# Spreading the weights of four V pairs by one set of copies in a decode kernel

## The chip, the cores and the metric

The kernel runs on one core of one Trainium2 chip. The metric is device time in microseconds (us) of one execution. Executions of one kernel agree within about 0.1% (before: 1342.69 to 1343.98 us). The profiles abbreviate the engines: PE is TensorE, PEld its weight loads, DVE is VectorE, ACT is ScalarE, POOL is GpSimd, SP is SyncE, which issues the loads. L516 is line 516 of the kernel that ran, so the same line has other numbers in other kernels.

## The reference, cut to what matters

One decode step of attention over a long cache is mixed with a small MLP. What matters here is the attention:

```python
# k_cache, v_cache: 4 batches x 32 heads x 8192 keys x 128, bf16: 268 MB each
scores = jnp.einsum("bhqd,bhkd->bhqk", q, k_cache) * (Dh ** -0.5)
p = _softmax(scores, axis=-1)
o = jnp.einsum("bhqk,bhkd->bhqd", p, v_cache)
```

Each byte of K and V is used once. Everything else (`wq`, `wo`, the MLP weights) is some 39 MB.

## The kernel before

The work is cut into 32 "pairs" of K and 32 of V. One pair is four heads of one batch, 8.39 MB, loaded into two of the five slots of a ring. Eight pairs make a group, which has one softmax. The V pairs run eight pairs behind the K pairs, so in the long middle part TensorE alternates: a K pair, a V pair, a K pair, and so on. Behind the last K pair, the last eight V pairs follow one another.

```python
order = []
for d in range(ND):
    order += [("k", d)] + [("v", d - LAG)] * (d >= LAG)
order += [("v", d) for d in range(ND - LAG, ND)]
```

In the profiles `TB` holds transposed K (the work of VectorE), `S_ps` the scores, `o_ps` the sums of the V matmuls and `OS` a scaled copy of them, which ScalarE begins behind every second V pair ("the OS activation").

The softmax of a group leaves its exponentials, transposed, in the tile `PT`. They are the weights of the V matmuls, but a V matmul needs them in a wide, mostly zero layout. The tile `PB` holds that layout for four V pairs (`NW = 4` slots), and `spread_p` copies one pair's weights from `PT` into its slot, with two copies on ScalarE and two on GpSimd:

```python
def spread_p(d):
    g, t = divmod(d, GD)                      # group, pair in the group (GD = 8)
    lo = RD * (d % NW)                        # slot of PB
    Pv = PT_t[g][:, :, RD * t:RD * t + RD].rearrange("p (q j) i -> p i q j", j=4)
    Bv = PB[:, lo:lo + RD].rearrange("p i z w s j -> p i (z w) s j")
    for q in range(NQ):
        at = slice(QP * q, QP * (q + 1))
        if q % 2 == 0:
            nc.scalar.copy(out=Bv[at, :, :, q, :], in_=Pv[at])
        else:
            nc.gpsimd.tensor_copy(out=Bv[at, :, :, q, :], in_=Pv[at])
```

Behind a softmax it is called for three pairs of the new group (four for the first). In `v_pair`, a slot is filled again as soon as its V pair is done, for the pair that comes four later:

```python
def v_pair(d):
    ...                                        # cut: load of V, 64 matmuls with PB[slot d % NW]
    if tv == GV - 1:
        sum_up(d, g, t, b, h0)
    if t < GD - NW:
        spread_p(d + NW)
    if t == GD - 1 and d + 1 < ND:
        spread_p(d + NW)
```

## Time and profile before

| | before |
|---|---|
| time, median of 6 runs | 1343.07 us (1342.69 to 1343.98) |
| bytes read, mean rate | 575.68 MB, 429 GB/s |
| busy share of the DMA queue that loads | 99.6% of 16 engines |
| TensorE, VectorE busy | 1050.9 us (78%), 638.2 us (48%) |
| ScalarE, GpSimd busy | 66.2 us, 71.4 us (5% each) |
| of these the copies of `spread_p` | 39.6 us, 38.9 us (64 copies on each) |

The table is read from the bottom: the edited operations are 3% of the span on each of two engines that idle 95% of it. The lines themselves are shown in the prediction.

### The profile page before, as it was taken

The page shows a single profiled execution, that of the slowest core. Times are in us where ns is not written, and L with a number is a line of the kernel's source. Part 1 is how long each engine was busy: PE and PEld are TensorE (multiplying, and loading weights), DVE is VectorE, ACT ScalarE, POOL GpSimd, SP SyncE. Part 2 cuts the span into 40 slices and gives each one's busy share as a digit, 9 for nine tenths or more (in the row PEclk, how much of TensorE's full clock was granted, in tenths as well). Part 3 has the DMA queues.
Part 4 walks back from the last instruction along what each step waited for, and adds up shares of the span by engine and source line. Part 5 has one row for each costly group of instructions (what it writes and reads, how often), then busy time and mean ns, then how long its engine had stood idle before and what let it go on. Part 6 is the DMA issues. An engine that isn't in the chain of part 4 may idle for free.

```text
span 1341.0 us, 6872 instructions
## 1 busy us (share of the span) xinstructions
PE 1050.9 (78%) x4550; PEld 138.3 (10%) x1396; DVE 638.2 (48%) x386; ACT 66.2 (5%) x99; POOL 71.4 (5%) x209
## 2 busy tenths in 40 slices
PE   2665877887778788787879778789697879898888
PEld 0000000001001010101001010101011011111111
DVE  2555988556544347454436256646145556100000
ACT  0000000200000000100000000100000000111000
POOL 2000000100000001000000000100000000100000
PEclk9687999898988998888989898899898889889899
DMA  9999999999999999999999999999999999999998
GB/s 415 438 430 435 436 436 424 441 429 428 436 434 428 443 430 423 442 429 435 434 435 428 433 438 434 436 421 431 434 434 438 434 421 440 432 426 431 426 427 340
DMA packets 15466, 576.13 MB, mean 430 GB/s; under 512 B 1726, under 2 KB 1990, under 8 KB 3148
## 3 DMA queue, kind: packets, MB, share of 16 engines
q1 hardware_dynamic: 15428, 575.69, 99.6%
q8 instruction: 23, 0.38, 0.1%
q14 instruction: 7, 0.06, 0.0%
q10 hardware_dynamic: 8, 0.00, 0.0%
HBM read 575.68 MB, written 0.01 MB: 429 GB/s over the span
## 4 chain that ended last, share of the span: by engine, by line
DMA 62%; DVE 24%; PE 12%; another core or an unknown queue 1%; issue 0%; ACT 0%; SPq 0%; DVEq 0%
DMA ring<-in_A_k_cache_dram 51%; DVE TB L456 21%; PE o_ps L540 9%; DMA ring<-in_A_v_cache_dram 7%; DMA ring<-in_A_wo_dram 2%; DVE OS L561 2%; DMA x<-in_gate_w_dram 2%; PE S_ps L461 1%; PE acc L286 1%; DVE mx L483 0%; PE S_ps L320 0%; PE led L577 0%; PE o_ps L320 0%; DVE PT L497 0%
## 5 line engine op out<-in xcount | busy, mean ns | idle before, releaser
L456 DVE STREAM_TRANSPOSE TB<-ring 128x2048 uint32<-128x2048 uint32 x256 | 568.2, 2278 | 474.2 <-DMA ring<-in_A_k_cache_dram 467.1
L461 PE MATMUL S_ps<-TB,Z 128*128 128x512 bf16 x1990 | 524.3, 412 | 198.1 <-DVE TB L456 183.9
L540 PE MATMUL o_ps<-ring,PB 128*64 128x512 bf16 x2048 | 465.1, 389 | 49.8 <-DMA ring<-in_A_v_cache_dram 48.5
L461 PEld LDWEIGHTS <-Z 128*128 128x128 bf16 x512 | 53.0, 103 | 654.4 <-issue 654.4
L540 PEld LDWEIGHTS <-PB 128*64 128x64 bf16 x512 | 57.4, 112 | 450.9 <-issue 450.3
L516 POOL COPY PB<-PT 32x256 bf16<-32x256 bf16 x64 | 38.9, 608 | 711.3 <-PE o_ps L540 518.4
L569 DVE SCALAR_TENSOR_TENSOR OS<-o_ps,mE,OS 128x512 f32<-128x512 f32 x5 | 3.8, 751 | 139.1 <-ACT OS L567 139.1
L514 ACT COPY PB<-PT 32x256 bf16<-32x256 bf16 x64 | 39.6, 619 | 256.6 <-PE o_ps L540 250.7
L438 POOL COPY Z<-qa 32x4 bf16<-32x4 bf16 x128 | 25.6, 200 | 459.5 <-PE S_ps L461 433.3
L557 ACT ACTIVATE OS<-o_ps,mE 128x512 f32<-128x512 f32 x11 | 7.6, 687 | 451.9 <-PE o_ps L540 451.9
L561 DVE SCALAR_TENSOR_TENSOR OS<-o_ps,mE,OS 128x512 f32<-128x512 f32 x33 | 24.3, 737 | 1.5
L492 ACT ACTIVATE TB<-S_ps,mx 128x2048 bf16<-128x2048 f32 x4 | 7.9, 1967 | 332.0 <-DVE mx L489 332.0
L244 PE MATMUL S_ps<-identb,x 6*128 6x6 bf16 x8 | 0.6, 196 | 22.1 <-DMA x<-in_gate_w_dram 22.1
L286 PE MATMUL acc<-ring,hT 128*4 128x512 bf16 x56 | 13.6, 408 | 5.4 <-ACT TB L492 5.4
L286 PE MATMUL acc<-ring,LT 128*4 128x512 bf16 x64 | 15.1, 378 | 1.6 <-DMA ring<-in_A_wo_dram 1.0
L320 PE MATMUL o_ps<-ring,xw 128*4 128x512 bf16 x112 | 9.8, 471 | 4.9 <-DMA ring<-in_B_w_gate_dram 4.9
L577 PEld LDWEIGHTS o_ps<-selg,OS 128*128 128x128 f32 x88 | 11.5, 191 | 9.4 <-issue 9.0
L497 DVE STREAM_TRANSPOSE PT<-TB 128x2048 bf16<-128x2048 bf16 x4 | 9.2, 2312 | 6.4 <-ACT TB L492 6.4
L483 DVE TENSOR_REDUCE mx<-S_ps 128x1 f32<-128x2048 f32 x4 | 9.1, 2282 | 6.2 <-PE S_ps L461 6.2
L577 PE MATMUL o_ps<-selg,OS 128*128 128x8 f32 x88 | 10.5, 245 | 0.0
L567 ACT ACTIVATE OS<-o_ps,mE 128x512 f32<-128x512 f32 x5 | 3.4, 687 | 128.2 <-PE o_ps L540 128.2
L589 DVE SCALAR_TENSOR_TENSOR OT<-led,sgb,rinv 128x8 bf16<-128x8 f32 x5 | 1.2, 237 | 16.2 <-PE led L577 16.2
(73 smaller groups left out, 81.8 us busy)
## 6 DMA issues: line engine op xcount, KB each, us to landing
ring<-in_A_v_cache_dram SPq DMA_DIRECT2D x18, 4096.0 KB, 30.0
ring<-in_A_k_cache_dram SPq DMA_DIRECT2D x14, 4096.0 KB, 29.8
ring<-in_A_v_cache_dram SPq DMA_DIRECT2D x6, 2048.0 KB, 39.5
ring<-in_B_w_gate_dram SPq DMA_DIRECT2D x1, 7168.0 KB, 37.0
ring<-in_B_w_up_dram SPq DMA_DIRECT2D x1, 7168.0 KB, 37.1
ring<-in_B_w_down_dram SPq DMA_DIRECT2D x1, 7168.0 KB
ring<-in_A_wo_dram SPq DMA_DIRECT2D x4, 1024.0 KB
ring<-in_A_v_cache_dram SPq DMA_DIRECT2D x4, 1024.0 KB, 30.3
```

Source lines behind the costliest of these rows:

```text
L286: nc.tensor.matmul(acc(n), lhsT=lhsT, rhs=rhs, start=start, stop=True, skip_group_check=True)
L320: nc.tensor.matmul(ps[32 * k:32 * k + Bn, z, :], lhsT=xT[TW * half + t], rhs=cols(w, t, 4 * z + k), start=(half + t == 0), stop=(half == 1 ...
L438: nc.gpsimd.tensor_copy(out=Z[at, :, QP - 1 + QP * q], in_=qa[at, :, h0 + q, b])
L456: nc.vector.transpose(out=flat_t.bitcast(U32).rearrange("p (j i) -> p j i", j=CJ), in_=kn[:, half].bitcast(U32))
L461: nc.tensor.matmul(sps[:, z, :], lhsT=Z[:, 2 * half + e, s:s + P], rhs=T[:, 16 * z:16 * z + 16, :, e], start=(t + n + half + e == 0), stop ...
L483: nc.vector.tensor_reduce(out=mx[:, 0:1], in_=sps[:].rearrange("p z n -> p (z n)"), axis=AX.X, op=ALU.max)
L497: nc.vector.transpose(out=PT[:].rearrange("p j i -> p (j i)"), in_=PTs)
L514: nc.scalar.copy(out=Bv[at, :, :, q, :], in_=Pv[at])
L516: nc.gpsimd.tensor_copy(out=Bv[at, :, :, q, :], in_=Pv[at])
L540: nc.tensor.matmul(o_ps[w // 2][row:row + NM, w % 2, :], lhsT=PB[:, RD * (d % NW) + n, z].rearrange("p w s j -> p (w s j)"), rhs=vn[:, j0 ...
L561: nc.vector.scalar_tensor_tensor(out=OS[:], in0=o_ps[w // 2][:, w % 2, :], scalar=mE[:, w:w + 1], in1=OS[:], op0=ALU.mult, op1=ALU.add)
L577: nc.tensor.matmul(oT, lhsT=OS[:, q * Dh:(q + 1) * Dh], rhs=selg[:, q].rearrange("p t s -> p (t s)"), start=(q == 0), stop=(q == 3), skip_ ...
```

## The change

The intent is fewer, larger copies. While K pairs still come, the weights of four V pairs are spread by one set of four copies: behind the first softmax, then behind the fourth and the eighth V pair of a group, when all four slots are free. Behind the last K pair, where no K pair lies between two V pairs, they are still spread pair by pair, except that the first three go together and the last two go together.

```diff
-            for i in range(NW):
-                if g == 0 or i < NW - 1:
-                    spread_p(GD * g + i)
+            if g == 0:
+                spread_p(0, NW)
+            elif g == NG - 1:
+                spread_p(GD * g, NW - 1)
...
-    def spread_p(d):
+    def spread_p(d, n=1):
...
-        Pv = PT_t[g][:, :, RD * t:RD * t + RD].rearrange("p (q j) i -> p i q j", j=4)
-        Bv = PB[:, lo:lo + RD].rearrange("p i z w s j -> p i (z w) s j")
+        Pv = PT_t[g][:, :, RD * t:RD * (t + n)].rearrange("p (q j) i -> p i q j", j=4)
+        Bv = PB[:, lo:lo + RD * n].rearrange("p i z w s j -> p i (z w) s j")
...
-            if q % 2 == 0:
+            if q % 2 == 0 and not (q and n == NW - 1):
...
-        if t < GD - NW:
-            spread_p(d + NW)
-        if t == GD - 1 and d + 1 < ND:
-            spread_p(d + NW)
+        if g == NG - 1:
+            if t < 2:
+                spread_p(d + NW)
+            if t == 3:
+                spread_p(d + NW - 1, 2)
+        elif t == NW - 1:
+            spread_p(d + 1, NW)
+        elif t == GD - 1:
+            if g + 1 < NG - 1:
+                spread_p(d + 1, NW)
+            else:
+                spread_p(d + NW)
```

More of the change, by code (lines that the diff above doesn't have):

```diff
@@ L146 @@
     NW = GD // 2
+    NG = ND // GD
     HV = GV * NQ
```

## The prediction

> **What bounds the kernel now.** I read the page from the top: busy shares first, then the strip of the span, the DMA queues and the chain, then the groups of the lines that the change edits, and last the timeline around the copies.
>
> ```profile
> PE 1050.9 (78%) x4550; PEld 138.3 (10%) x1396; DVE 638.2 (48%) x386; ACT 66.2 (5%) x99; POOL 71.4 (5%) x209
> DMA  9999999999999999999999999999999999999998
> GB/s 415 438 430 435 436 436 424 441 429 428 436 434 428 443 430 423 442 429 435 434 435 428 433 438 434 436 421 431 434 434 438 434 421 440 432 426 431 426 427 340
> q1 hardware_dynamic: 15428, 575.69, 99.6%
> HBM read 575.68 MB, written 0.01 MB: 429 GB/s over the span
> DMA 62%; DVE 24%; PE 12%; another core or an unknown queue 1%; issue 0%; ACT 0%; SPq 0%; DVEq 0%
> ```
>
> The reader is to see that no compute engine is near full, while the DMA digit is 9 in every slice but the last, and one queue is busy for 99.6% of 16 engines' span. The bytes are fixed: 575.69 MB at 429 GB/s over the span are 1341 us, the span itself. The table by stretches agrees: every stretch I asked for up to 1330 us has a DMA share of 1.00 or 1.01, only the last 11 us have 0.48. So the kernel streams the K and V caches, and time comes down only if the stream gets faster or its last 11 us shorter.
>
> The chain puts 24% on VectorE and 12% on TensorE, which looks like something to win. It isn't. The chain follows what set each transfer's issue: a ring slot came free, the queue issued, the data landed some 30 us later. One pair is 4 heads x 8192 x 128 x 2 B = 8.39 MB, or 19.5 us at 430 GB/s; of 30 us to landing, about 10 us are spent behind an older transfer. The issue was thus about 10 us early, and moving it by less costs nothing. ScalarE has 0% of this chain, and GpSimd does not appear in it.
>
> The edited lines:
>
> ```profile
> L516 POOL COPY PB<-PT 32x256 bf16<-32x256 bf16 x64 | 38.9, 608 | 711.3 <-PE o_ps L540 518.4
> L514 ACT COPY PB<-PT 32x256 bf16<-32x256 bf16 x64 | 39.6, 619 | 256.6 <-PE o_ps L540 250.7
> L438 POOL COPY Z<-qa 32x4 bf16<-32x4 bf16 x128 | 25.6, 200 | 459.5 <-PE S_ps L461 433.3
> L540 PE MATMUL o_ps<-ring,PB 128*64 128x512 bf16 x2048 | 465.1, 389 | 49.8 <-DMA ring<-in_A_v_cache_dram 48.5
> ```
>
> Each V pair has four copies, two on ScalarE and two on GpSimd: 32 x 2 = 64 on each, 39.6 and 38.9 us busy. They wait for TensorE (PB frees when the V matmuls are done); the V matmuls wait for the V data (48.5 of their 49.8 us idle). One view puts 8.0 us of two V weight loads, at 1181.3 and 1249.2 us, down to these GpSimd copies; but those had ended at 1150.0 and 1202.2, and the same two loads also wait for V data, which the matmuls behind them show (3.10 and 2.74 us). The timeline shows why the copies are hidden:
>
> ```profile
> 678.88 14.00 PE L540 MATMUL o_ps<-ring,PB 128*64 128x512 bf16 x64
> 692.94 1.23 POOL L516 COPY PB<-PT 32x256 bf16<-32x256 bf16 x2 [33.70 <-PE o_ps L540]
> 693.07 1.24 ACT L514 COPY PB<-PT 32x256 bf16<-32x256 bf16 x2
> 720.01 14.00 PE L540 MATMUL o_ps<-ring,PB 128*64 128x512 bf16 x64
> ```
>
> The columns are start, duration, engine, what. One V pair ends at 692.9, its copies take 1.2 us, and the next V pair starts at 720.0, because the order alternates: a K pair lies between.
>
> [...] of eight GpSimd copies at 241.6 us (5.22 us, 0.65 each), beside VectorE's transposes, none took noticeably longer, while one copy of the 64 took 973 ns; at 1145.6 a VectorE cast of x lies beside six copies that need 4.27 us[...].
>
> **The change part by part.** The instruction order that both kernels build to shows it: ACT falls from 47 rows to 41, POOL from 63 to 56, and TensorE, VectorE and the DMA queue keep their sequences, row for row. On TensorE only waits differ: up to V pair 20 the weight loads now wait for ACT and POOL ahead of pairs 0, 4, 8, 12, 16 and 20, where before they did ahead of 0, 8 and 16 (and for ACT ahead of 1, 9 and 17).
>
> *Steady part (V pairs 0 to 23).* Removed: 24 x 4 copies of 256 elements per partition. Added: six sets (after the first softmax and behind V pairs 3, 7, 11, 15, 19), each of four copies of 1024. [...] GpSimd: the 16-element copy of line 438 takes 200 ns and the 256-element one 608, so (608 - 200) / 240 = 1.70 ns per element, and 200 + 1.70 x 1008 = 1.91 us each. ScalarE: 48 x 0.62 = 29.8 us become 12 x 1.91 = 22.9. GpSimd: 48 x 0.61 = 29.2 become 22.9.
>
> *Last group (V pairs 24 to 31).* Behind the last softmax three pairs are spread at once: one copy of 768 on ScalarE (1.5 us), three on GpSimd (3 x 1.5 = 4.5 us, where six took 4.27). Pairs 27, 28 and 29 stay as they are; 30 and 31 go together behind V pair 27 (two copies of 512 on each engine, 1.04 us each). ScalarE: 9.9 us become 1.5 + 3.7 + 2.1 = 7.3. GpSimd: 9.7 become 4.5 + 3.7 + 2.1 = 10.3.
>
> Sum: ScalarE 39.6 to about 30.2 us, GpSimd 38.9 to about 33.2. None of it is on the path that sets the end, so the direct gain is 0 us.
>
> *What becomes tighter.* Between V pairs 3 and 4, say, four pairs' weights used to be ready long before; now the set starts when V pair 3 ends, and V pair 4 needs it. ScalarE has the OS activation first (0.69 us), then two copies: 0.69 + 2 x 1.91 = 4.5 us. The gaps in TensorE's V matmuls at these five places in the trace before are 24.8 to 27.8 us; for the first set, 15.2 us lie between the PT transpose (241.5) and the first V matmul (256.75). Even if the K data is there at once, the K pair keeps TensorE busy for 15 us (733.9 to 749.0). So at least 10 us of margin remain. In the tail, V pair 24 starts at 1181.3, some 31 us after its weights would be ready (1145.7 + 4.5 = 1150.2); V pairs 30 and 31 are written by about 1249.4 and pair 30 starts at 1288.2.
>
> **The rivals.** *A wait of TensorE for PB takes the place of the removed copies.* For it: only four slots of weights exist, all four are now free and filled at once, and every set hangs on a single V pair's end. If the K pair were not between, six waits of 4.5 us would cost up to 27 us of TensorE time, and the time would be near 1350 us after the queue's 10 us of slack absorbed part. Against it: the order of instructions on TensorE shows the K pair's matmuls in each of these gaps, and the margin above.
>
> *Long GpSimd copies block VectorE, which frees ring slots later.* For it: a copy is now three times as long. Against it: [...] the trace has them beside copies with no change. Only the sum of the two halves in the tail (line 571[...], at 1248.3) may meet the pair's copy (1246.6 to 1248.7): 0.4 us, in a stretch where TensorE then waits for V data anyway. Worth 0.
>
> *Fewer instructions and semaphores make the whole faster.* For it: 13 rows fewer. Against it: ACT and POOL idle 95% of the span. Worth under 1 us.
>
> **Range and chances.** The predicted time is that of before, 1343.0 us. Three runs of before spread over 1.3 us; the DMA rate in slices moves by some GB/s[...]. I choose 1340 to 1347: 3 us below for a lucky stream, 4 above for a small stall I overlooked. A change of 2% is 27 us, more than the first rival's worst sum. Faster by over 2%: 0.01; within 2%: 0.98; slower: 0.01.
>
> **What would show each step right or wrong.** DMA still at 99.6% and 429 GB/s or so. ACT busy near 57 us, POOL near 66 (66.2 - 9.4 and 71.4 - 5.7). Copies of 1024 elements at 1.8 to 2.0 us; if they took over 5 us, the slope would be wrong. V matmuls with no idle time put down to PB, ACT or POOL, the gaps behind V pairs 3, 7, 11, 15 and 19 still 24 us or more. The prediction would be wrong if the wait for V weights showed several us at these places, if the transposes' mean rose over 2278 ns, or if the DMA strip fell below 9 in any inner slice.

The sum came to about 30.2 us on ScalarE (from 39.6) and 33.2 us on GpSimd (from 38.9), with a direct gain of 0 us. GpSimd's terms come from the 200 and 608 ns of the trace. With GpSimd's slope put on ScalarE's measured 619 ns, an estimate from the trace before alone is 619 + 768 x 1.70 = 1925 ns, and 12 x 1.925 = 23.1 us in place of ScalarE's 22.9. In the second rival, "them" are VectorE's transposes; that only the sum of the two halves may meet a GpSimd copy was the author's estimate. The 10 us of slack are an estimate, from 30 us to landing and 19.5 us for a transfer alone; the runs below put it at some 3 to 13.

## The result, and the profile after

The changed kernel took 1343.27 us (median of 6 runs, 1343.11 to 1344.04), the kernel before 1343.07 us. The ratio is 1.0001, with a 95% interval of 0.9988 to 1.0014: the same. (A ratio here is the mean time of one kernel's fast runs over that of the other's fast runs of the same rounds, so it is not quite the ratio of the quoted medians.)

These are the page's lines of the changed kernel: busy times, the strip of the DMA share (one digit for each fortieth of the span, in tenths), the loading queue, and the chain of work that ended last.

```profile
PE 1049.8 (78%) x4550; PEld 139.1 (10%) x1396; DVE 638.5 (48%) x386; ACT 57.2 (4%) x56; POOL 65.7 (5%) x168
...
DMA  9999999999999999999999999999999999999998
...
q1 hardware_dynamic: 15428, 575.69, 99.6%
...
DMA 65%; DVE 23%; PE 10%; another core or an unknown queue 1%; issue 0%; ACT 0%; SPq 0%; DVEq 0%
```

ScalarE lost 43 instructions and 9.0 us of work, GpSimd 41 instructions and 5.7 us. TensorE and VectorE did the same work in the same time, the queue is busy for the same 99.6%, and ScalarE still has no part in the chain.

The groups of the copies, with each shape apart (columns: count, then busy us, mean ns of one, then the engine's idle time ahead of them and what ended it):

```profile
L516 ACT COPY PB<-PT 32x1024 bf16<-32x1024 bf16 x12 | 23.0, 1918 | 2.5 <-DVE PT L498 2.4
L518 POOL COPY PB<-PT 32x1024 bf16<-32x1024 bf16 x12 | 22.8, 1899 | 285.6 <-PE o_ps L542 257.4 <-DVE PT L498 28.0
L518 POOL COPY PB<-PT 32x768 bf16<-32x768 bf16 x3 | 4.7, 1576 | 77.0 <-DVE PT L498 76.9
L516 ACT COPY PB<-PT 32x512 bf16<-32x512 bf16 x2 | 2.1, 1058 | 0.0
```

A copy of four times the elements takes 3.1 times as long (1918 against 619 ns), which is where the saving comes from. The place that the prediction showed, V pairs 11 and 12, now reads so in the timeline (start, duration, engine):

```profile
692.57 0.69 ACT L568 ACTIVATE OS<-o_ps,mE 128x512 f32<-128x512 f32 x1 [76.90 <-PE o_ps L542]
693.03 3.79 POOL L518 COPY PB<-PT 32x1024 bf16<-32x1024 bf16 x2 [49.03 <-PE o_ps L542]
693.15 3.82 ACT L516 COPY PB<-PT 32x1024 bf16<-32x1024 bf16 x2
...
720.18 5.15 PE L542 MATMUL o_ps<-ring,PB 128*64 128x512 bf16 x23
```

The set is done at 697.0 and the V pair that needs it starts at 720.2, as before (720.0). The weights used to be ready three V pairs ahead; now they are ready 23 us ahead. That is what the change spends: not time, but margin. Over the five sets behind a V pair, TensorE's gap is 25.8, 24.8, 27.2, 27.1 and 28.4 us, and a set is done 4.0 to 4.1 us into it.

### The profile page after: what moved, and what is told of

Same layout as the page of the kernel before. It is cut to its first block, busy times and chain, and to the rows that moved or that the text cites. A ratio compares the mean times of both kernels' runs of the same rounds, so it can differ in the third digit from the quotient of the medians.

```text
span 1341.4 us, 6794 instructions
## 1 busy us (share of the span) xinstructions
PE 1049.8 (78%) x4550; PEld 139.1 (10%) x1396; DVE 638.5 (48%) x386; ACT 57.2 (4%) x56; POOL 65.7 (5%) x168
## 3 DMA queue, kind: packets, MB, share of 16 engines
q1 hardware_dynamic: 15428, 575.69, 99.6%
## 4 chain that ended last, share of the span: by engine, by line
DMA 65%; DVE 23%; PE 10%; another core or an unknown queue 1%; issue 0%; ACT 0%; SPq 0%; DVEq 0%
DMA ring<-in_A_k_cache_dram 51%; DVE TB L457 20%; DMA ring<-in_A_v_cache_dram 10%; PE o_ps L542 8%; DMA ring<-in_A_wo_dram 2%; DVE OS L572 2%; DMA x<-in_gate_w_dram 2%; PE S_ps L462 1%; PE S_ps L321 0%; PE o_ps L321 0%; DVE PT L498 0%; DVE mx L484 0%; PE acc L287 0%; PE led L588 0%
## 5 line engine op out<-in xcount | busy, mean ns | idle before, releaser
L457 DVE STREAM_TRANSPOSE TB<-ring 128x2048 uint32<-128x2048 uint32 x256 | 568.1, 2278 | 474.3 <-DMA ring<-in_A_k_cache_dram 467.3
L518 POOL COPY PB<-PT 32x1024 bf16<-32x1024 bf16 (+3 forms) x23 | 33.2, 1444 | 455.3 <-PE o_ps L542 349.8
L516 ACT COPY PB<-PT 32x1024 bf16<-32x1024 bf16 (+3 forms) x21 | 30.3, 1444 | 25.9 <-PE o_ps L542 20.9
L493 ACT ACTIVATE TB<-S_ps,mx 128x2048 bf16<-128x2048 f32 x4 | 7.9, 1967 | 332.0 <-DVE mx L490 332.0
L287 PE MATMUL acc<-ring,hT 128*4 128x512 bf16 x56 | 15.1, 439 | 5.4 <-ACT TB L493 5.4
L245 PE MATMUL S_ps<-identb,x 6*128 6x6 bf16 x8 | 0.6, 196 | 22.5 <-DMA x<-in_gate_w_dram 22.5
```

Of the source, the lines that this page charges most:

```text
L287: nc.tensor.matmul(acc(n), lhsT=lhsT, rhs=rhs, start=start, stop=True, skip_group_check=True)
L457: nc.vector.transpose(out=flat_t.bitcast(U32).rearrange("p (j i) -> p j i", j=CJ), in_=kn[:, half].bitcast(U32))
```

## The experiments

"The same" does not tell why. Two quite different reasons are possible. Either nothing that ScalarE and GpSimd do can move this time, because the stream from HBM sets it. Or the copies could move it and are hidden, by the K pair that lies between two V pairs and by transfers that the queue holds ready. The experiments enlarge the set, take it away, give the same copying back to the kernel before, take the stream's bound away, and take the K pair away. Each ran beside the kernel before on the same chip, whose medians in the three sessions were 1343.62, 1343.27 and 1342.91 us.

### No steady copies at all

```diff
     def spread_p(d, n=1):
+        if n == NW and d > 0:
+            return
```

> The changed kernel without the five steady sets of copies (V pairs 4 to 23 use the weights of pairs 0 to 3, so the result is wrong on purpose). Theory (the copies lie beside a K pair and the stream sets the time): 1343 us, within 0.15%. Rival (copies on ScalarE and GpSimd still cost something[...]): 3 us or more faster, since 19 us of copies on each of two engines and ten waits are gone.

Measured: 1343.31 us, ratio 0.9998 (0.9983 to 1.0013). V pairs 4 to 23 then use stale weights, so the result is wrong by construction; the comparison with the reference did not flag it, which says only that its tolerance does not see these weights. ScalarE was busy for 38.6 us, 19 less than in the changed kernel, and no time came of it. So no way of making these copies cheaper can gain more here than the noise, which leaves room for some 2 us; the changed kernel had nothing to win.

### The sets four, eight, sixteen and ten times over

The sets behind V pairs 3, 11 and 19 are copied again and again into the same place (the result stays right):

```diff
-        for q in range(NQ):
+        for q in list(range(NQ)) * (4 if n == NW and d % GD == NW else 1):   # 4, 8, 16, 10
```

> The changed kernel with the sets behind V pairs 3, 11 and 19 copied four times over (about 15.4 us on GpSimd and 16 us on ScalarE for each set, where one takes 3.8 and 4.5). The gap between the two V pairs is 25 to 28 us. Theory of the hidden set: TensorE waits 0 us for the weights, 1343 us, within 0.15%. Rival (the set is already on the path): 3 x 11.5 = 34 us slower, or near 10 us slower if the queue absorbs part.

> The same sets copied eight times over (about 31 us each). Theory: this is more than the gap of 25 to 28 us, so TensorE's V pair starts 4 to 7 us later at three places, but the DMA queue holds some 10 us of transfers ahead, so the time is 1343 to 1347 us. If the queue had no such slack: 12 to 21 us slower. If the gap were not what hides the copies: no wait at all.

> The same sets copied sixteen times over (about 62 us each). Theory: the V pair starts some 36 us later at three places, the queue absorbs 10 of them, so 3 x 26 = 78 us slower: 1421 us, 1400 to 1440. Rival (the stream sets the time whatever ScalarE and GpSimd do): 1343 us.

| times over | one set on GpSimd | TensorE's V matmuls waited for copies | time | ratio to before |
|---|---|---|---|---|
| 1 (the change) | 3.8 us | 0 | 1343.27 us | 1.0001 |
| 4 | 15.8 us | 0 | 1343.47 us | 0.9998 |
| 8 | 31.6 us | 6.4 + 4.5 + 4.5 = 15.4 us | 1343.67 us | 1.0007 |
| 16 | 62.9 us | 37.9 + 35.5 + 35.8 = 109.1 us | 1430.22 us | 1.0643 |

At four times the set still fits into the gap. At eight times it doesn't, and TensorE's waits in the trace name the copies:

```profile
PE o_ps L542 <- POOL PB L518: 15.4, 3, 6.4
```

(columns: us in total, times, the longest). The time of three runs hardly moved. One of the four, the profiled one, did take 1347.56 us, and its stretch from 1037 to 1050 us, behind the third set, shows a DMA share of 0.82, which I read as a wait longer than what the queue held ahead. At sixteen times both covers are used up. The rate strip of the page has three holes, at 139, 110 and 123 GB/s, one behind each large set:

```profile
GB/s 415 437 437 427 447 422 434 435 433 432 429 430 139 432 420 437 435 420 441 432 428 110 380 439 417 439 435 435 424 433 359 123 435 434 445 422 431 425 428 354
...
q1 hardware_dynamic: 15428, 575.69, 93.7%
```

So the first reason falls: ScalarE's and GpSimd's copies can move the time. Of 109.1 us of waiting, 1430.22 - 1343.62 = 86.6 us reached the end, so 22.5 us were absorbed, on average 7.5 for each set. I had put that slack at 10 us. To see whether it is a fixed slack or a share, I ran ten times, and eight times again with more rounds:

> The changed kernel with the sets behind V pairs 3, 11 and 19 copied ten times over (about 39.5 us each). From the two runs at eight and sixteen times: TensorE waited 6.4, 4.5 and 4.5 us at a set of 31.6 us, so 14.3, 12.4 and 12.4 us here, 39.1 in all. At sixteen times 109.1 us of waiting cost 86.6 us, so the queue absorbed 22.5 us, 7.5 for each set. Theory (a fixed slack per set): 39.1 - 22.5 = 16.6 us slower, 1360 us, 1355 to 1365. Rival (a share of each wait is absorbed, 21%): 31 us slower, 1374 us.

> The kernel with eight-fold sets once more, with five rounds, because one of its four runs took 1347.6 us where the others took 1343.4 to 1343.7. Theory (the wait of 4.5 to 6.4 us is just inside the slack of some 7.5): most runs at 1343 to 1344.5 us, a few up to 1348. If the slack were smaller than that: a median above 1345.

Ten times: 1359.35 us (1358.77 to 1363.0), 16.4 us above the kernel before (ratio 1.0127). TensorE waited 37.6 us for the copies, and 37.6 - 22.5 = 15.1: a fixed slack, not a share. Eight times again: 1345.02 us (1344.23 to 1347.33), ratio 1.0018 with an interval from 1.0005. That misses the expectation: the median lies above the line that I had drawn, though no wait in its trace is longer than 6.5 us.

The traces tell why: the slack is not 7.5 us at each place. How much later than in the changed kernel do V pairs 11, 19 and 23 start, each well behind one of the large sets?

| times over | waits for the three sets | V pairs 11, 19, 23 start later by | so absorbed at each set |
|---|---|---|---|
| 10 | 14.0, 11.3, 12.2 us | 0.6, 9.2, 16.0 us | 13.4, 2.7, 5.4 us |
| 16 | 37.9, 35.5, 35.8 us | 24.6, 56.7, 87.0 us | 13.3, 3.3, 5.5 us |

(For the second set at ten times: 11.3 - (9.2 - 0.6) = 2.7. The last column is from the unrounded times.) The two runs agree: some 13, 3 and 5.5 us. The rate strip at ten times shows it too. It has holes behind the second and the third set, 338 and 323 GB/s, and none behind the first, although TensorE waited longest there (the other three lines are the V pairs that waited, the wait in brackets):

```profile
GB/s 423 441 431 418 444 433 422 442 431 424 441 433 421 425 433 431 431 433 431 435 433 338 437 431 431 424 438 430 435 423 441 323 433 435 431 431 432 429 426 354
...
422.78 15.77 PE L542 MATMUL o_ps<-ring,PB 128*64 128x512 bf16 x64 [14.03 <-POOL PB L518]
...
733.00 15.96 PE L542 MATMUL o_ps<-ring,PB 128*64 128x512 bf16 x64 [11.34 <-POOL PB L518]
...
1051.51 15.44 PE L542 MATMUL o_ps<-ring,PB 128*64 128x512 bf16 x64 [12.15 <-ACT PB L516]
```

So in the second run at eight times the wait of 6.5 us for the first set was free; those of 3.8 and 4.4 us for the second and the third left V pair 19 1.1 us and V pair 23 1.7 us late, and the time was some 2 us longer. Why the three places differ was not tested.

### The same copying in the kernel before

Here the kernel before makes the copies of the very same twelve V pairs sixteen times over, but pair by pair:

```diff
-        for q in range(NQ):
+        for q in list(range(NQ)) * (16 if d % GD >= NW and d < ND - GD else 1):
```

> The kernel before with the very copies of the same twelve V pairs (4 to 7, 12 to 15, 20 to 23) also made sixteen times over, but pair by pair as it has them (about 20 us behind each of the V pairs 0 to 3, 8 to 11, 16 to 19, needed three V pairs later). The amount of copying added is that of the changed kernel with sixteen-fold sets. Theory (what counts is the time between the copy and its use): 1343 us, within 0.2%. Rival (so much copying disturbs the transposes or the transfers by itself): slower by 10 us or more, and the mean of the transposes over 2278 ns.

Measured: 1343.4 us, ratio 1.0002 (0.9986 to 1.0017). The groups show how much copying that is:

```profile
L514 ACT COPY PB<-PT 32x256 bf16<-32x256 bf16 x424 | 264.7, 624 | 206.1 <-PE o_ps L540 191.6 <-DVE PT L497 4.8
L516 POOL COPY PB<-PT 32x256 bf16<-32x256 bf16 x424 | 257.5, 607 | 553.1 <-PE o_ps L540 338.9 <-DVE PT L497 191.5
L456 DVE STREAM_TRANSPOSE TB<-ring 128x2048 uint32<-128x2048 uint32 x256 | 568.4, 2278 | 474.3 <-DMA ring<-in_A_k_cache_dram 467.1 <-PE S_ps L461 7.1
```

ScalarE had 225 us more to do than in the unaltered kernel before. The changed kernel at sixteen times had only 173 us more than its own 57.2, yet lost 87 us where this one lost none. The amount of copying in the whole kernel is thus not what counts, but how much of it must be done between one V pair and the next that needs it. Two things differ here from the sixteen-fold sets, and the run does not separate them: the weights are ready three V pairs ahead, and they come in pieces of some 21 us, most of which fit into one gap anyway. The transposes keep their 2278 ns beside 424 GpSimd copies, so they are not slowed either.

### Less V to load

Both kernels load only a quarter of the bytes of 29 V pairs (wrong result):

```diff
-            vs = load_pair(vv, RING, apart=d >= ND - GD + 2)
+            vs = [ring[:, slots(1)] for _ in range(2)]
+            for half in range(2):
+                nc.sync.dma_start(out=vs[half][:, 0:RING // 4], in_=vv[:, half * RING:half * RING + RING // 4])
```

> The kernel before with only a quarter of the bytes of 29 of the 32 V pairs loaded (wrong result on purpose): 182.5 MB less, so the stream alone would need about 915 us and TensorE and VectorE become the bound. Expected 1080 to 1200 us. It is the base for the changed kernel with the same cut.

> The changed kernel with the same cut of V bytes. Theory (a set takes about 4.5 us and the K pair between keeps TensorE busy for 15 us or more even when no data is late): the same as the kernel before with this cut, within 0.5%. Rival 1 (the set is hidden only by TensorE's waits for data): about 5 x 4.5 = 22 us slower. Rival 2 (fewer instructions pay once the stream is not the bound): faster by 5 us or more.

Measured: 1188.55 us (1185.12 to 1188.89) for the kernel before, 1187.24 us (1187.1 to 1188.45) for the changed one; their ratios to the uncut kernel before are 0.8841 and 0.8839. The loading queue is busy for 79.1% of 16 engines, so the stream is no longer full, and no V matmul waits for V data in either trace. The two kernels are still the same within the spread. The gaps behind V pairs 3, 7, 11, 15 and 19 shrink to 19.7, 26.5, 21.1, 26.5 and 20.4 us, still four times the set or more. So the set is hidden even where V data is never late. (K data still is: VectorE waits 281.7 us for it, so a K pair with no wait at all was not reached at these five places. Elsewhere in this trace it was: V pairs 3 and 13 start 15.0 us after the V pair before them ended, the prediction's 15 us.) Nor do fewer instructions pay where the stream is not full.

### Four at once in the last group too

```diff
             if g == 0:
                 spread_p(0, NW)
-            elif g == NG - 1:
-                spread_p(GD * g, NW - 1)
...
         if g == NG - 1:
-            if t < 2:
-                spread_p(d + NW)
             if t == 3:
-                spread_p(d + NW - 1, 2)
+                spread_p(d + 1, NW)
         elif t == NW - 1:
             spread_p(d + 1, NW)
         elif t == GD - 1:
-            if g + 1 < NG - 1:
-                spread_p(d + 1, NW)
-            else:
-                spread_p(d + NW)
+            spread_p(d + 1, NW)
```

> The changed kernel with four pairs at once in the last group too: one set behind V pair 23 and one behind V pair 27, where no K pair lies between. Theory: V pairs 24 and 28 wait for their weights, ScalarE's 1.4 us of OS activations and two copies of 1.9 us, so they start 2 to 2.5 us later than in the changed kernel (about 1183.5 and 1251.5 us), and the stream hides it: 1343 to 1345 us. Rival (a wait in the tail goes straight to the end): 4 to 5 us slower.

Here a set stands between two V pairs with no K pair between, and TensorE does wait for it:

```profile
1182.22 3.48 PE L540 MATMUL o_ps<-ring,PB 128*64 128x512 bf16 x8 [4.76 <-ACT PB L514]
...
1253.13 3.02 PE L540 MATMUL o_ps<-ring,PB 128*64 128x512 bf16 x8 [4.77 <-ACT PB L514]
```

The two V pairs start at 1182.2 and 1253.1 us, where I expected 1183.5 and 1251.5. In the changed kernel the same two places wait for V data, 3.8 and 2.7 us, and start at 1181.5 and 1249.5. Measured: 1343.13 us over five runs, ratio 0.9998 (0.9986 to 1.0011). So two exposed sets of 4.8 us cost nothing either: part replaces a wait for data that was there anyway, and the rest is made up before V pair 30, which starts at 1288.3 us (1288.4 in the changed kernel). The care that the change takes with the last group is not needed for the time, as long as nothing else uses up that slack.

No experiment points to a kernel faster than these two, since even with no steady copies at all the time is the same.

## Why the prediction was right

**The bound.** That the stream is full and the compute hidden held: 99.6% and 429 GB/s before and after, and with less V to load the time fell by 11.6%.

**The cost of the copies.** GpSimd's copy of 1024 elements was estimated at 1.91 us, from two sizes in the trace before, and measured 1.899 us. ScalarE's was put at 1.91 us too, with a fixed part that was not measured, and measured 1.918 us. From the sizes 256 and 1024 the slope is now (1918 - 619) / 768 = 1.69 ns per element on ScalarE and (1899 - 602) / 768 = 1.69 on GpSimd, for copies that read PT with a step of 64 bytes. Activations of ScalarE that read the scores and the sums of V without a step took less per element: 1967 ns for 2048, 687 for 512. That the step is the cause was not tested. ScalarE was estimated at 57 us busy and measured 57.2, GpSimd at 66 and 65.7. One statement was loose: 47 to 41 and 56 against 63 are rows of a listing that merges like neighbours. In instructions, 43 and 41 went, not 6 and 7. The sum was done per copy and did not depend on it.

**The margin.** "At least 10 us" held: the set is done 4.1 us into gaps of 24.8 us or more, and behind the first softmax 11 us ahead (245.6 against 256.9). No V matmul waits for a copy. The view that put 8.0 us of two weight loads down to GpSimd copies puts 8.7 us there now, at the same V pairs 24 and 28, and their matmuls still wait for V data (3.78 and 2.74 us).

**The rivals.** The first, a wait of TensorE for the new sets, was rejected because a K pair lies between. Shown: a set up to four times as long still fits, and the set does cost TensorE time where no K pair lies between. Its "near 1350 us" does not come out of its own numbers (1343 + 27 - 10 is 1360 if the slack counts once, and 1343 if each wait has its own) and was never put to the test as such. The nearest runs are the second one at eight times, with three waits of 3.8 to 6.5 us, 1345.02 us, and the two sets exposed at the end, 1343.13. Its 27 us are also no less than the 2% (26.9 us) that they were said to be under. The second, GpSimd copies that hold VectorE up, came out at the predicted place: the sum of two halves behind V pair 27 took 0.98 us where the others take 0.69, beside the larger GpSimd copy. No other group of VectorE instructions has a mean more than 8 ns above the one before (the transposes 2278 ns in both).

```profile
1246.78 2.14 POOL L518 COPY PB<-PT 32x512 bf16<-32x512 bf16 x2 [30.70 <-PE o_ps L542]
...
1248.48 0.98 DVE L582 TENSOR_TENSOR OS<-OS,TB 128x512 f32<-128x512 f32 x1
1249.45 1.89 PE L542 MATMUL o_ps<-ring,PB 128*64 128x512 bf16 x8 [2.74 <-DMA ring<-in_A_v_cache_dram]
```

The matmul after it waits for V data, so those 0.3 us are hidden, as predicted. GpSimd copies are longer in such places too. The one that lies beside VectorE's cast of x took 1816 ns where its like took 1449 and 1464; the kernel before has the same 0.37 us there (973 against some 600 ns), the copy that the prediction names. In the run with four at once in the last group, two GpSimd copies beside that sum took 2.24 us, where the copies just ahead of them took 1.90 and 1.92. These instructions lie side by side in the traces; what one does to the other was not tested. The third, a gain from fewer instructions, is zero with the stream full and within the spread without.

**One size was off.** The slack of the queue was taken as 10 us from landing times (30 us from issue to landing, 19.5 for a transfer alone). Two sizes of waits show some 13, 3 and 5.5 us at three places. A median over all issues could give the order of the slack, but not that one place has less than a third of it. The prediction's range did not rest on the difference.

## What to carry to other kernels

If one resource is busy for 99% of the span, ask of a change not what it saves but what margin it spends. Merging copies trades lead time for fewer instructions: the same copying, sixteen-fold, was free pair by pair with three V pairs of lead, and cost 87 us in sets with one K pair of lead. Enlarge the suspected cost step by step until the time moves: that measures each cover (here some 25 us of K pair, then 3 to 13 us of queued transfers), where a single "no change" cannot tell hidden from harmless. And look at each place by itself: an average slack of 7.5 us had me expect that waits of 4.5 us are free; at a place that holds 3 us, even 3.8 were not.
